# A weight conversion's integer scaling and a second value product given to GpSimd, with the converting periods in another order

## The chip, the cores and the metric

The kernel runs on one core of a Trainium2 chip. The metric is the time of one execution on the device in microseconds (us), as the median of several runs. A profile of one execution stands beside it, with every instruction's start and duration on TensorE (PE in the profile), VectorE (DVE), ScalarE (ACT), GpSimd (POOL) and the DMA queue of SyncE (SP).

## What is computed

The reference has two parts. The first is a threshold attention over 8 batches, 8 heads, 576 positions and 64 dimensions: scores are `q k^T / 8`; scores below the row's maximum less `tau` are dropped; what stays goes through exp, is divided by its row sum and multiplies `v`. The second part takes the result as 4608 rows of 512 and computes `relu(x @ w_in)**2 @ w_out` with `w_in` of 512 x 2048 and `w_out` of 2048 x 512.

```python
scores = scale * np.matmul(q, k.transpose(0, 1, 3, 2))
thresh = np.max(scores, axis=-1, keepdims=True) - tau
scores = np.where(scores >= thresh, scores, -1000000000.0)
attn = np.exp(scores - np.max(scores, axis=-1, keepdims=True))
attn = attn / (np.sum(attn, axis=-1, keepdims=True) + 1e-09)
h = np.maximum(x @ w_in, 0.0)     # x: the attention's output, heads side by side
out = (h * h @ w_out)
```

The two weight matrices arrive as float64 (they are made by multiplying float32 numbers by a float64 factor), so the kernel reads them as pairs of 32-bit words, a low and a high one, and makes float32 numbers of them with integer arithmetic.

## The kernel before, in words

The kernel has two stages. The attention goes first, in *periods*; the matrix products of the second part follow (lines 1117 to 1187), where a scheme of sums and differences of blocks saves products. The change touches the attention's periods alone.

**Periods.** Heads are taken in 32 pairs, and the query rows of two pairs make 9 units of 128 rows, 144 units in all. One call of `period(p)` (line 608) handles units A = 2p and B = 2p + 1: for each unit and each head j of the pair it makes scores (`SA`, `SB`), takes the row's extreme while it copies the scores from PSUM to SBUF (`topA0`, `topA1`, `topB0`, `topB1`, line 452, VectorE), makes the threshold on GpSimd (`leastA`, `leastB`, line 459, only 128x2 numbers), the exponentials on ScalarE (`powA0` and so on, line 462) and the mask with its row sum on VectorE (`maskA0` and so on, line 467: it reads the scores and the exponentials, both in SBUF). `over` (line 474, GpSimd) adds the small constant to the row sums of the period before and `inv` (line 477, VectorE) inverts them.

The same call works on earlier units too: `U`, `V` and `W` transpose the masked weights on TensorE into PSUM, `eU`, `eV` and `eW` copy them out on ScalarE (line 523); `W` also spreads the inverted sums (line 515). `PV` multiplies them by the values (line 532), and `x` takes the two heads' products out of PSUM: where no weights are converted, VectorE multiplies each by the inverted sums on the way (line 644). `T` and `eT` transpose a new pair's queries or keys (lines 398, 403 and 411).

**Conversion.** In periods 2 to 34 the kernel also converts 32 chunks of weights, one begun in each of periods 2 to 33 (`converts`, line 583). A chunk is 128 partitions of 512 numbers. `c1` (line 205, ScalarE) takes the magnitude of the high words, `c2` (line 212, ScalarE) scales the low words' integers in place, `c3` (line 219, GpSimd) clamps the magnitude, `c4` (line 227, VectorE) shifts and masks it, `c5` (line 235, VectorE) joins it with the high words' upper bits, `c6` (line 245, GpSimd) adds the scaled low words. `c1` and `c2` work on the chunk that the period begins, `c3` to `c6` on that of the period before. In converting periods `x` is split: ScalarE copies head 0's product (line 642) and GpSimd multiplies it later (`xm`, line 654), VectorE multiplies head 1's on the way out.

**Order.** Each engine runs its instructions in program order, and the program order within a period is a list of step names written out by hand: `PLAIN` (line 592) for periods without conversion, `CONVERTING` (line 597) for those with it. So one list sets the queue of every engine. Before the change, a converting period gives:

- VectorE: topA1 topA0 topB0 topB1 maskA1 inv maskA0 x(head 1) c4 maskB1 c5 maskB0
- GpSimd: over leastA leastB c3 c6 xm
- ScalarE: eU c1 c2 powA1 powA0 eV powB1 powB0 x(head 0) eT eW
- TensorE: U SA SB V PV T W

`touch` (line 355) adds waits between engines that use the same PSUM bank: the scores of unit A and `PV` share banks 0 and 5, the scores of unit B and `W` share banks 2 and 3, `T` and the last 64 keys of the scores share banks 1 and 4; `U` and `V` share one buffer.

Of the kernel before, what the change touches and what calls it, by code (L numbers as in the profile page):

```python
# [12 lines left out]
U32 = mybir.dt.uint32  # L13
ALU = mybir.AluOpType
AF = mybir.ActivationFunctionType
# [33 lines left out]
def kernel(  # L49
# [25 lines left out]
    nc = tc.nc  # L75
    B, H, S, D = q.shape
    P = 128
# [131 lines left out]
    def convert2(m):  # L209
        if m in parts:  # L210
            lo = parts[m][0]
            nc.scalar.activation(out=lo, in_=lo.bitcast(U32), func=AF.Copy, bias=0.0, scale=2.0**-29)

    def convert3(m):
        if m not in parts:
            return
        a = parts[m][2].bitcast(FP32)
        low, high = (0x38000000, 0x47EFFFFF)
        nc.gpsimd.tensor_scalar(  # L219
            out=a, in0=a, scalar1=as_float(high), scalar2=as_float(low), op0=ALU.min, op1=ALU.max  # L220
        )

    def convert4(m):
        if m not in parts:
            return
        lo, hi, a = parts[m]
        nc.vector.tensor_scalar(
            out=a, in0=a, scalar1=3, scalar2=0x3FFFFFFF, op0=ALU.logical_shift_left, op1=ALU.bitwise_and
        )
# [255 lines left out]
    wT = {}  # L485

    TURNS = {}
    for g in range(2, 2 * len(pairs)):
        two, x = divmod(g - 4, 4)
# [4 lines left out]
    SCALE_AT = 10  # L494
# [4 lines left out]
    def fill(m, f, pt, at=None):  # L499

        first, count = FILLS[f]
        if m not in wT:
            wT[m] = sb.tile([P, (2 * CH + 2) * P], FP32, tag="wT", bufs=W_RING, name="wT")
        for i, (u, c) in enumerate(FIRST[first : first + count]):
            half_turn(pt, i, weights[2 * m + u][:, c, :, :].rearrange("p j d -> p (j d)"), at)
        if f == "W":
            rs = smalls.pop(m)
            for j in range(2):
                for r in range(2):
                    rows = ds(r * HALF, HALF)  # L510
                    for u in range(2):
                        one = rs[rows, 3, 2 * u + j : 2 * u + j + 1]
                        wide = bass.AP(tensor=one.tensor, offset=one.offset, ap=[one.ap[0], [0, D]])
                        to = pt[ds(u * D, D), r, ts(count + j, HALF)]
                        made = nc.tensor.matmul(to, wide, ident[rows, rows], start=True, stop=True)  # L515
                        touch("turns", made, at and at + r * BANK, BANK)

    def filled(m, f, pt, at=None):

        first, count = FILLS[f]  # L520
        count += 2 * (f == "W")
        to = wT[m][:, ds(weight_at(first) * P, count * P)]
        touch("weights", nc.scalar.copy(joined(to), whole(pt, 0, count)), at, 2 * BANK, m)  # L523
# [15 lines left out]
    def valued(m):  # L539

        for u in range(2):
            n = 2 * m + u
            weights.pop(n)
            if units[n][1] == FULL:
                for i in units[n][0]:
                    loaded_v.pop(i)
                    if i + 3 < len(pairs):
                        load_v(i + 3)
# [10 lines left out]
    def has(n):  # L559
        return 0 <= n < NU  # L560
# [13 lines left out]
    def ask(every=True):  # L574

        while given:
            to, from_ = given.popleft()
            nc.sync.dma_start(out=to, in_=from_)
        for _ in range(len(later) if every else min(1, len(later))):
            to, from_ = later.popleft()  # L580
            nc.sync.dma_start(out=to, in_=from_)

    def converts(p):
        return is_wide and (has_chunk(p) or has_chunk(p - 1))

    def has_chunk(p):
        return p in starts

    def begun(n):
        return starts.get(n)  # L590
# [4 lines left out]
        maskB1  # L595
    """.split()
    CONVERTING = """
        fetch U SA s1 eU over topA1 topA0 leastA SB c1 topB0 V c2 PV topB1 powA1 powA0
        eV powB1 maskA1 T leastB inv c3 powB0 W maskA0 x c4 maskB1 c5 maskB0 c6 xm eT eW
    """.split()  # L600

    def spots():
        return [(sc[:, ds(b * BANK + REST, (FULL + 1) * HALF)], b * BANK) for b in (1, 4)]

    def middle():
        return sc[:, 2 * BANK : 4 * BANK].rearrange("p (r n) -> p r n", r=2)

    def period(p):

        A, B_, a, b = 2 * p, 2 * p + 1, 2 * p - 2, 2 * p - 1  # L610
        m, turns = p - 2, TURNS.get(p, ())
        late, pt = {"W": []}, {}

        def fills(f, m):
            if has(2 * m):
                pt[f] = pt_pool.tile([P, 2, BANK], FP32, tag="pt", name="pt")
                fill(m, f, pt[f])

        def evict(f, m):
            if has(2 * m):  # L620
                filled(m, f, pt[f], 2 * BANK if f == "W" else None)

        def W():
            if has(2 * m + 2):
                pt["W"] = middle()
                fill(m + 1, "W", pt["W"], 2 * BANK)

        def turn_some():
            late["turn"] = [turn(g // 2, g % 2, spots()) for g in turns]

        def PV():
            if has(2 * m):
                values(m)

        def values_out():
            if not has(2 * m):
                return
            late["x"] = x = sb.tile([P, 2, P], FP32, tag="x", bufs=2, name="x")
            for j in range(2):
                from_ = sc[:, ds(5 * j * BANK, P)]  # L640
                if converts(p) and j == 0:
                    made = nc.scalar.copy(x[:, j, :], from_)
                else:
                    made = nc.vector.tensor_tensor(  # L644
                        out=x[:, j, :], in0=from_, in1=wT[m][:, ts(SCALE_AT + j, P)], op=ALU.mult
                    )
                touch("x", made, 5 * j * BANK, P, m)

        def given_out():
            if has(2 * m):  # L650
                x = late.pop("x")
                if converts(p):
                    mine = x[:, 0, :]
                    nc.gpsimd.tensor_tensor(out=mine, in0=mine, in1=wT[m][:, ts(SCALE_AT, P)], op=ALU.mult)
                wT.pop(m)
                valued(m)
                give_x(m, x)
            ask(False)

        def scored_a():  # L660
            if has(A):
                scores(A, False)
                scores(A, True)
                scores(B_, True)
                softmax(A)

        def scored_b():
            if has(A):
                scores(B_, False)
                softmax(B_)  # L670

        def every(key):
            for then in late.get(key, ()):
                then()

        steps = {
            "U": lambda: fills("U", m), "V": lambda: fills("V", m + 1), "W": W, "T": turn_some,
            "eU": lambda: evict("U", m), "eV": lambda: evict("V", m + 1), "eW": lambda: evict("W", m + 1),
            "eT": lambda: every("turn"),
            "SA": scored_a, "SB": scored_b,  # L680
            "PV": PV, "x": values_out, "xm": given_out,
            "c1": lambda: convert1(begun(p)), "c2": lambda: convert2(begun(p)),
            "c3": lambda: convert3(begun(p - 1)), "c4": lambda: convert4(begun(p - 1)),
            "c5": lambda: convert5(begun(p - 1)), "c6": lambda: convert6(begun(p - 1)),
            "s1": lambda: sums_due(p) and sums_step(), "s2": lambda: sums_due(p) and p < 60 and sums_step(), "fetch": lambda: fetch(begun(p + 2)),
        }
        steps["over"] = lambda: do(a, "over")
        steps["inv"] = lambda: do(a, "inverse")
        for letter, n in (("A", A), ("B", B_)):
            for what, name in (("least", "least"),):  # L690
                steps[what + letter] = lambda n=n, name=name: do(n, name)
            for what, name in (("top", "top"), ("pow", "power"), ("mask", "mask")):
                for j in range(2):
                    steps[f"{what}{letter}{j}"] = lambda n=n, name=name, j=j: do(n, name, j)
        for name in CONVERTING if converts(p) else PLAIN:
            steps[name]()
        for n in (A, B_):
            if has(n) and units[n][1] == FULL:
                for i in units[n][0]:
                    turned.pop(i)  # L700
# [489 lines left out]
def as_float(bits):  # L1190
    import struct

    return struct.unpack("<f", struct.pack("<I", bits))[0]
# [30 lines left out]
```

## Time and profile before

| what | value |
|---|---|
| median of 3 runs | 1316.72 us (1316.07 to 1317.4) |
| the profiled execution's own time | 1314.57 us |
| span of its trace | 1312.8 us |
| busy share of the span: PE, DVE, ACT, POOL | 97%, 77%, 65%, 66% |
| converting periods | 33, from about 30 us to 269 us of the span |
| time of one converting period in the trace | 7.26 us (`inv` starts at 152.22 and 159.48 us) |

The shares are averages over two stages with different limits: the second stage, from about 520 us, keeps TensorE busy almost without a gap, and in the attention VectorE and ScalarE are as busy as TensorE. A row of a timeline gives the start, the duration, the engine, the line of the kernel, the operation, and in square brackets how long the engine had been idle and for whom it waited. Durations of neighbours on VectorE and ScalarE overlap at their ends, so the distance from start to start is what an instruction takes of its engine.

### The profile page before, as it was taken

Reading aid. Unit: us, or ns where it says so; the run is one execution under the profiler, and the core shown is the slowest. Engines: PE = TensorE matmul, PEld = TensorE weight load, DVE = VectorE, ACT = ScalarE, POOL = GpSimd, SP = SyncE. Lnnn points to the kernel's source line nnn. Section 1 sums busy time; section 2 is a strip of 40 time slices with the busy share of each in tenths; the row PEclk is TensorE's granted clock in tenths of the full one; section 3 lists DMA queues with packets and bytes.
Section 4 is the critical chain, followed back from the end, with each engine's and each line's share of the span. In section 5 each row is a group of like instructions: output and inputs, shape, how many; then the busy total and the mean of one; then the engine's idle time right before and its main releaser. Section 6 shows DMA issues by size and latency. Waiting matters only on the chain.

```text
span 1312.8 us, 47885 instructions
## 1 busy us (share of the span) xinstructions
PE 1271.9 (97%) x19483; PEld 1142.1 (87%) x19483; DVE 1007.1 (77%) x2464; ACT 855.8 (65%) x1497; POOL 872.0 (66%) x991
## 2 busy tenths in 40 slices
PE   8998989899999999999999999999999999999998
PEld 5666666677777777999999999999999999999998
DVE  5999999999999996877887788777656654665463
ACT  6999999988999986566756675665524322432240
POOL 1556555565555421778887888758777777777775
PEclk9999999999999999999999999999999999999999
DMA  5465566544433312466556655669745224522411
GB/s 150 105 176 153 153 177 179 153 113 103 99 78 84 79 42 47 148 209 198 183 184 209 200 188 176 194 229 387 260 161 161 63 99 162 161 65 97 161 33 33
DMA packets 247035, 192.12 MB, mean 146 GB/s; under 512 B 97184, under 2 KB 195488, under 8 KB 246816
## 3 DMA queue, kind: packets, MB, share of 16 engines
q1 hardware_dynamic: 245504, 188.66, 47.6%
q8 instruction: 153, 2.51, 0.8%
q14 instruction: 66, 0.54, 0.1%
q10 hardware_dynamic: 1312, 0.41, 0.1%
HBM read 116.65 MB, written 72.35 MB: 144 GB/s over the span
## 4 chain that ended last, share of the span: by engine, by line
PE 74%; DVE 7%; issue 6%; ACT 3%; POOL 3%; DMA 3%; SPq 0%; POOLq 0%; DVEq 0%; ACTq 0%
PE ph L825 30%; PE po L960 29%; PE sc L532 6%; PE sc L434 5%; DVE arena L452 4%; PE pt L380 3%; POOL arena L219 2%; DVE arena L467 2%; ACT arena L462 1%; ACT arena L523 1%; DVE arena L235 1%; PE sc L398 1%; DMA xT<-arena 1%; PE sc L515 1%; DMA wall<-w 1%
## 5 line engine op out<-in xcount | busy, mean ns | idle before, releaser
L125 POOL TENSOR_TENSOR arena<-arena 128x512 f32<-128x512 f32 (+1 forms) x314 | 378.1, 1223 | 133.6 <-DVE arena L125 115.8
L960 PE MATMUL po<-wall,arena 128*128 128x128 f32 x3528 | 394.8, 275 | 1.4 <-ACT arena L737 1.4
L960 PEld LDWEIGHTS po<-wall,arena 128*128 128x128 f32 x3528 | 394.3, 192 | 1.9 <-ACT arena L737 1.8
L825 PE MATMUL ph<-arena,wall 128*128 128x128 f32 x3528 | 394.2, 275 | 0.7 <-DVE arena L644 0.7
L825 PEld LDWEIGHTS ph<-arena,wall 128*128 128x128 f32 x3528 | 394.0, 192 | 0.8 <-issue 0.8
L125 DVE TENSOR_TENSOR arena<-ph,arena 128x512 f32<-128x512 f32 x378 | 256.4, 689 | 86.2 <-PE ph L825 65.4
L122 POOL TENSOR_TENSOR arena<-arena 128x128 f32<-128x128 f32 (+2 forms) x314 | 254.8, 812 | 49.1 <-DMA arena<-w 32.9
L125 DVE TENSOR_TENSOR arena<-po,arena 128x128 f32<-128x128 f32 x378 | 108.4, 290 | 167.8 <-PE po L960 163.4
L467 DVE SCALAR_TENSOR_TENSOR arena<-arena 128x576 f32<-128x576 f32 x288 | 229.5, 818 | 0.7 <-POOL arena L459 0.5
L462 ACT ACTIVATE arena<-arena 128x576 f32<-128x576 f32 x288 | 207.9, 772 | 15.6 <-DVE arena L452 11.4
L452 DVE TENSOR_SCALAR_CACHE_REDUCE arena<-sc 128x576 f32<-128x576 f32 x288 | 205.4, 751 | 15.8 <-ACT arena L523 4.6
L771 ACT COPY c<-arena 128x512 f32<-128x512 f32 (+1 forms) x303 | 174.0, 581 | 50.2 <-DVE arena L122 41.5
L532 PEld LDWEIGHTS sc<-arena 64*64 64x64 f32 x5760 | 153.7, 133 | 50.1 <-DVE arena L452 37.2
L532 PE MATMUL sc<-arena 64*64 64x128 f32 (+1 forms) x5760 | 169.8, 262 | 19.4 <-DVE arena L452 18.8
L122 DVE TENSOR_TENSOR arena<-arena,c 128x512 f32<-128x512 f32 (+1 forms) x267 | 175.1, 664 | 6.2 <-ACT c L771 4.1
L434 PE MATMUL sc<-arena 64*64 64x64 f32 (+1 forms) x2304 | 167.1, 414 | 6.7 <-ACT arena L403 4.0
L523 ACT COPY arena<-pt 128x1024 f32<-128x1024 f32 x144 | 146.1, 1015 | 27.0 <-PE pt L380 26.7
L737 ACT COPY arena<-po 128x128 f32<-128x128 f32 x63 | 16.7, 265 | 186.2 <-PE po L960 183.4
L459 POOL TENSOR_SCALAR arena<-arena,tau_p 128x2 f32<-128x2 f32 x144 | 74.8, 520 | 81.1 <-DVE arena L452 77.9
L380 PEld LDWEIGHTS pt<-ident,arena 64*128 64x128 f32 x2304 | 83.4, 138 | 43.9 <-ACT arena L523 27.5
L737 ACT COPY arena<-ph 128x512 f32<-128x512 f32 x63 | 36.7, 582 | 123.5 <-PE ph L825 122.9
L380 PE MATMUL pt<-ident,arena 64*128 64x64 f32 x2304 | 102.6, 228 | 5.9 <-ACT arena L523 4.7
(50 smaller groups left out, 892.0 us busy)
## 6 DMA issues: line engine op xcount, KB each, us to landing
g<-arena SPq DMA_DIRECT2D x144, 256.0 KB, 2.6
arena<-g SPq DMA_DIRECT2D x144, 256.0 KB, 4.4
w<-arena SPq DMA_DIRECT2D x60, 256.0 KB, 2.4
wall<-w SPq DMA_DIRECT2D x49, 256.0 KB, 5.2
arena<-w SPq DMA_DIRECT2D x44, 256.0 KB, 3.3
arena<-in_v_dram SPq DMA_DIRECT2D x32, 288.0 KB, 3.8
out_dram<-arena SPq DMA_DIRECT2D x70, 128.0 KB, 2.2
arena<-in_q_dram SPq DMA_DIRECT2D x64, 128.0 KB, 3.5
```

What stands on the lines that cost most here:

```text
L122: e.tensor_tensor(out=out, in0=x, in1=y, op=ALU.subtract)
L125: e.tensor_tensor(out=out, in0=x, in1=y, op=ALU.add)
L380: made = nc.tensor.transpose(pt[:, r, ts(slot, HALF)], of[rows, :], ident[rows, rows])
L434: made = nc.tensor.matmul(sc[at, ds(to, count)], lhs, kT[rows, ds(at_k, count)], start=True, stop=True)
L452: made = nc.vector.tensor_scalar(out=s[:, j, :], in0=sc[:, ds(at, S)], scalar1=1.0, scalar2=None, op0=ALU.mult, op1=ALU.min, accum_out=nmx ...
L462: nc.scalar.activation(out=w[:, :, j, :], in_=of(j), func=AF.Exp, bias=nmx[:, j : j + 1], scale=-1.0)
L467: nc.vector.scalar_tensor_tensor(out=w[:, :, j, :], in0=of(j), scalar=thr[:, j : j + 1], in1=w[:, :, j, :], op0=ALU.is_le, op1=ALU.mult, a ...
L523: touch("weights", nc.scalar.copy(joined(to), whole(pt, 0, count)), at, 2 * BANK, m)
L532: made = nc.tensor.matmul(sc[ds(u * D, D), ds(5 * j * BANK + row, count)], loaded_v[i][rows, (c - (u != j)) % CH, :], wT[m][rows, ds(weigh ...
L771: nc.scalar.copy(c, y)
L825: nc.tensor.matmul(to[:, j, :], W_IN[m, k][:, ts(j, P)], of[k][:, m - 1, :], start=(not more and j == 0), stop=True, skip_group_check=True,)
L960: nc.tensor.matmul(to, g[:, j, :], w[:, j, :], start=(not more and j == 0), stop=(j == 3), skip_group_check=True)
```

## The change

Four edits. `c2` becomes a GpSimd instruction with the same operands. In a converting period ScalarE copies both heads' products out of PSUM, and GpSimd's `xm` multiplies both (256 columns) by the inverted sums. `c3` clamps the chunk that the period itself begins, so it runs a period sooner than `c4`, which stays where it is. And the list `CONVERTING` has another order.

```diff
@@ convert2
-            nc.scalar.activation(out=lo, in_=lo.bitcast(U32), func=AF.Copy, bias=0.0, scale=2.0**-29)
+            nc.gpsimd.tensor_scalar(out=lo, in0=lo.bitcast(U32), scalar1=2.0**-29, scalar2=None, op0=ALU.mult)
@@ the order
     CONVERTING = """
-        fetch U SA s1 eU over topA1 topA0 leastA SB c1 topB0 V c2 PV topB1 powA1 powA0
-        eV powB1 maskA1 T leastB inv c3 powB0 W maskA0 x c4 maskB1 c5 maskB0 c6 xm eT eW
+        fetch SA U eU T SB topA0 s1 c1 topA1 topB0 c3 V PV leastA over powA0 topB1
+        powA1 powB0 c4 eT inv x maskA1 maskA0 W leastB maskB0 c5 eV c2 powB1 c6 eW maskB1 xm
     """.split()
@@ values_out
-                if converts(p) and j == 0:
+                if converts(p):
                     made = nc.scalar.copy(x[:, j, :], from_)
@@ given_out
                 if converts(p):
-                    mine = x[:, 0, :]
-                    nc.gpsimd.tensor_tensor(out=mine, in0=mine, in1=wT[m][:, ts(SCALE_AT, P)], op=ALU.mult)
+                    both = x[:, :, :].rearrange("p j n -> p (j n)")
+                    nc.gpsimd.tensor_tensor(out=both, in0=both, in1=wT[m][:, ds(SCALE_AT * P, 2 * P)], op=ALU.mult)
@@ steps
-            "c3": lambda: convert3(begun(p - 1)), "c4": lambda: convert4(begun(p - 1)),
+            "c3": lambda: convert3(begun(p)), "c4": lambda: convert4(begun(p - 1)),
```

The queues of a converting period after the change:

- VectorE: topA0 topA1 topB0 topB1 c4 inv maskA1 maskA0 maskB0 c5 maskB1
- GpSimd: c3 leastA over leastB c2 c6 xm
- ScalarE: eU c1 powA0 powA1 powB0 eT x(head 0) x(head 1) eV powB1 eW
- TensorE: SA U T SB V PV W

`convert2` has a second caller, `convert_out` (line 1057), but the list it works through is empty with these sizes (`EARLY` is 16, and there are 16 blocks).

## The prediction

> **What bounds the kernel now.** I read the page's first lines, then busy time by stretches, then the timelines of the engines in one converting period.
>
> ```profile
> span 1312.8 us, 47885 instructions
> ...
> core 0: us, PE busy (x) PEld busy (x) DVE busy (x) ACT busy (x) POOL busy (x), PEclk, DMA share, GB/s
> 140.00:180.00 40.00, 35.88 (x934) 25.31 (x930) 38.52 (x112) 39.47 (x69) 24.04 (x34) 1.00 0.63 171
> ```
>
> The second row names the columns. In these 40 us of converting periods ScalarE is busy 39.47, VectorE 38.52, TensorE 35.88 and GpSimd 24.04. So ScalarE and VectorE both look full, and shares can't say which of them sets the pace. VectorE's timeline of one period can.
>
> ```profile
> 151.48 0.82 DVE L467 SCALAR_TENSOR_TENSOR arena<-arena 128x576 f32<-128x576 f32 x1
> ...
> 152.22 0.17 DVE L477 RECIPROCAL arena<-arena 128x4 f32<-128x4 f32 x1
> 152.31 0.79 DVE L467 SCALAR_TENSOR_TENSOR arena<-arena 128x576 f32<-128x576 f32 x1
> ...
> 153.03 0.29 DVE L644 TENSOR_TENSOR arena<-sc,arena 128x128 f32<-128x128 f32 x1
> 153.61 0.43 DVE L227 TENSOR_SCALAR arena<-arena 128x512 int32<-128x512 int32 x1 [0.29 <-POOL arena L219]
> ...
> 153.95 0.81 DVE L467 SCALAR_TENSOR_TENSOR arena<-arena 128x576 f32<-128x576 f32 x1
> ...
> 155.29 0.81 DVE L467 SCALAR_TENSOR_TENSOR arena<-arena 128x576 f32<-128x576 f32 x1
> ...
> 156.03 0.75 DVE L452 TENSOR_SCALAR_CACHE_REDUCE arena<-sc 128x576 f32<-128x576 f32 x1
> ...
> 158.74 0.81 DVE L467 SCALAR_TENSOR_TENSOR arena<-arena 128x576 f32<-128x576 f32 x1
> ...
> 159.48 0.17 DVE L477 RECIPROCAL arena<-arena 128x4 f32<-128x4 f32 x1
> ```
>
> From `inv` (L477) to `inv` is 159.48 - 152.22 = 7.26 us. Everything follows its forerunner at once, except `c4` (L227), which waits 0.29 us for GpSimd's `c3`. VectorE's own work is thus 6.97 us. Two of its terms matter later: a mask (L467) takes 0.74 from start to start (155.29 to 156.03), and the four tops (L452) take 2.71 (156.03 to 158.74, where the next mask starts).
>
> ```profile
> 151.74 0.72 POOL L459 TENSOR_SCALAR arena<-arena,tau_p 128x2 f32<-128x2 f32 x1 [0.87 <-DVE arena L452]
> 152.43 1.15 POOL L219 TENSOR_SCALAR arena<-arena 128x512 f32<-128x512 f32 x1
> 155.46 1.54 POOL L245 TENSOR_TENSOR arena<-arena 128x512 int32<-128x512 int32 x1 [1.89 <-DVE arena L235]
> 156.97 0.45 POOL L654 TENSOR_TENSOR arena<-arena 128x128 f32<-128x128 f32 x1
> 157.51 0.23 POOL L474 TENSOR_SCALAR arena<-arena 128x4 f32<-128x4 f32 x1
> 157.83 0.29 POOL L459 TENSOR_SCALAR arena<-arena,tau_p 128x2 f32<-128x2 f32 x1
> ```
>
> GpSimd's `c3` (L219) comes behind `leastB` (L459), which waits for the last top: that is why `c4` waits. ScalarE follows:
>
> ```profile
> 155.41 0.73 ACT L205 ACTIVATE arena<-arena 128x512 f32<-128x512 f32 x1
> 156.00 0.73 ACT L212 ACTIVATE arena<-arena 128x512 int32<-128x512 uint32 x1
> 156.83 1.46 ACT L462 ACTIVATE arena<-arena 128x576 f32<-128x576 f32 x2
> ```
>
> `c2` (L212) ends at 156.73, and the powers start at 156.83, just after VectorE's first top (156.03 + 0.75 = 156.78). ScalarE is nearly full, but it follows VectorE. TensorE does too: a gap of 0.62 us stands ahead of `PV` (L532), ended by a top:
>
> ```profile
> 153.44 0.71 PE L380 MATMUL pt<-ident,arena 64*128 64x64 f32 x16
> 154.08 2.18 PE L434 MATMUL sc<-arena 64*64 64x512 f32 x32
> ...
> 157.53 2.20 PE L532 MATMUL sc<-arena 64*64 64x128 f32 x72 [0.62 <-DVE arena L452]
> ```
>
> So **VectorE with GpSimd's `c3`** is the bound, and the converting stage is the only one that the change touches.
>
> **What GpSimd costs VectorE.** The profile holds a coupling that the chain of waits doesn't name. At the end of conversion, GpSimd adds weights with 512-column sums (L122, L125) while VectorE wants to mask.
>
> ```profile
> 270.44 1.82 DVE L467 SCALAR_TENSOR_TENSOR arena<-arena 128x576 f32<-128x576 f32 x1 [0.52 <-POOL arena L459]
> ...
> 277.58 1.10 DVE L467 SCALAR_TENSOR_TENSOR arena<-arena 128x576 f32<-128x576 f32 x1
> ...
> 290.82 0.81 DVE L467 SCALAR_TENSOR_TENSOR arena<-arena 128x576 f32<-128x576 f32 x1
> ```
>
> ```profile
> 270.37 1.28 POOL L122 TENSOR_TENSOR wall<-wall 128x512 f32<-128x512 f32 x1
> ...
> 276.79 1.28 POOL L125 TENSOR_TENSOR wall<-wall 128x512 f32<-128x512 f32 x1
> ...
> 289.69 1.29 POOL L125 TENSOR_TENSOR wall<-wall 128x512 f32<-128x512 f32 x1
> ```
>
> A mask, which reads two operands from SBUF, takes 0.81 alone. The one at 270.44 starts 0.07 after a GpSimd sum and takes 1.82: it is held 1.01 us, until 271.45, 0.20 before the sum's end (271.65). The one at 277.58 is held 0.29, until 277.87, again 0.20 before that sum's end (278.07). At 290.82 the sum ends only 0.16 later, and the mask isn't held. The reverse holds too: `leastB` issued during a mask takes 0.72, `leastA` during the tops (which read PSUM) 0.29. `leastB` at 151.74 ends at 152.46, 0.24 after the mask let go at 152.22. So **GpSimd's instructions and VectorE's masks exclude one another**: whoever starts first keeps the other out. The Trainium skill says so (SBUF — State Buffer, "SBUF: two separate sides": a GpSimd instruction and a VectorE one with two SBUF inputs take an exclusive lock, and the loser blocks); the trace agrees, save that the lock goes 0.20 us before GpSimd's recorded end.
>
> Read so, `c3`'s 1.15 us is mostly waiting: issued at 152.43 under a mask that lets go at 153.03, it ends at 153.58. That is 0.55 after the release, so some 0.60 us unhindered, an estimate (`leastB` loses 0.05 the same way: 0.24 against 0.29). `c6`, issued under the mask of 155.29, ends at 157.00, 0.97 after that mask let go (156.03).
>
> **The change, part by part.**
>
> ```profile
> L122 POOL TENSOR_TENSOR arena<-arena 128x512 f32<-128x512 f32 x134 | 170.5, 1273 | 10.2
> L122 POOL TENSOR_TENSOR arena<-arena 128x128 f32<-128x128 f32 x176 | 80.2, 458 | 38.7 <-DMA arena<-w 32.9
> L644 DVE TENSOR_TENSOR arena<-sc,arena 128x128 f32<-128x128 f32 x111 | 28.5, 286 | 6.5 <-issue 4.3 <-PE sc L532 1.8
> L227 DVE TENSOR_SCALAR arena<-arena 128x512 int32<-128x512 int32 x32 | 13.7, 427 | 9.5 <-POOL arena L219 9.5
> L212 ACT ACTIVATE arena<-arena 128x512 int32<-128x512 uint32 x32 | 22.8, 712 | 0.0
> L642 ACT COPY arena<-sc 128x128 f32<-128x128 f32 x33 | 8.2, 249 | 0.0
> ```
>
> *VectorE's second `x` goes*: 33 converting periods (the count of L642) by 0.286 us (L644) = 9.4 us.
>
> *`c4` no longer waits for `c3`*, which ran a period earlier: its idle time in the row, 9.5 us.
>
> *ScalarE* loses `c2` (32 x 0.71) and gets 33 more copies of 0.25: 39.47 busy us in 40 are 7.16 a period, so 6.7 are left. Nothing is counted for this, since VectorE sets the pace; ScalarE and TensorE (35.88 in 40, so 6.5 a period) merely have to keep under the new period. They do: with `PV` started at the second top's end (1.4 us into the period, counted from the first top), it ends at 3.6; the two copies end at about 4.0, the scores of unit A (under 1.4 of the 2.18 us of both, L434) at 5.4, `U` (0.7, L380) and `T` (8 or 10 of the transposes of which `U` has 16, so at most 0.4) at 6.5, while the next first top, which the bank rule now makes wait for `T`, is due at 7. What hides the reordered ScalarE work is this 0.5 us; if it went, the period would grow by what is missing.
>
> *`xm` doubles to 256 columns.* Sums of 128 and 512 columns (0.458 and 1.273) give 0.00212 us a column, so 0.73 instead of 0.45. It follows `c6` while VectorE does its tops, which hold nobody out.
>
> *`c3`, `leastA`, `over` now stand ahead of `inv`.* That is an added wait: `inv` and behind it all masks now queue on VectorE for GpSimd. Counted from the first top: `c6` ends at 0.97 as now, `xm` at 1.67, `c3` (0.60, under the tops, its magnitude being made by then) at about 2.3, `leastA` at 2.6; `over` starts between 2.5 and 2.85 (gaps between GpSimd instructions are -0.03 to 0.09 in the rows above) and lasts 0.23. `inv` could start at 2.71 + 0.34 (`c4`'s step, 153.61 to 153.95) = 3.05. So `over` just makes it. I count 0.04 us a period for brushes with `c4` and `leastB`: 1.3 us.
>
> *`c2` on GpSimd* isn't in the trace. It comes behind `leastB`, with masks on VectorE until `c6`. It therefore can't run without holding a mask: issued during `maskA1`, it gets its turn when that ends and holds `maskA0` until 0.20 before its own end. That a waiting GpSimd instruction is let in between two masks was seen once: an `xm` issued under a mask took 1.07, and the mask behind that one 1.01 instead of 0.81, held until 31.05, 0.19 before `xm`'s end.
>
> ```profile
> 30.85 1.01 DVE L467 SCALAR_TENSOR_TENSOR arena<-arena 128x576 f32<-128x576 f32 x1
> ```
>
> ```profile
> 30.17 1.07 POOL L654 TENSOR_TENSOR arena<-arena 128x128 f32<-128x128 f32 x1 [0.83 <-ACT arena L642]
> ```
>
> `c2`'s length unhindered is bounded by `c3` (one input, 512 columns: 0.60) and a 512-column sum (1.28); below nothing it can't be, since it must read its 512 columns. I take `c3`'s, the same operation on as many numbers: after the release 0.55, less 0.20, holds a mask 0.35 us. 32 x 0.35 = **11.2 us**. A full sum's hold was 1.01 us at 270.44, the upper end: 32.3 us. `c6`, two integer inputs, gives 0.97 - 0.20 = 0.77, the middle.
>
> The skill has a rule against this edit (Perfetto Trace Analysis, "Optimizing Scalar/DVE Operations": moving work between VectorE and GpSimd might not help, since they share a port). By it the edit is a loss that the other edits must pay for, and that is how the sum treats it.
>
> *DMA queue*: the loads of queries and keys (issued at `eT`) now precede `c6`'s store instead of following `xm`'s; each still waits for its own producer and is needed a period or more later, so 0.
>
> The sum: -9.4 - 9.5 + 11.2 + 1.3 = -6.4 us. A period goes from 7.26 to 7.07. The profiled execution took 1314.57 (its span and 1.77 around it), 2.15 below the median of the runs shown; I apply the difference to the median: 1316.72 - 6.4 = **1310.3 us**.
>
> **The rivals.**
>
> *`c2` is dear* (the slower end). Its numbers are read as unsigned integers, scaled as floats and written as integers, two conversions that `c3` lacks, and the words lie two apart. Masks lose what it holds; the saving of 18.9 - 1.3 = 17.6 us is used up at 17.6 / 32 = 0.55 us of hold, a length of 0.80. At `c6`'s hold (0.77) it is 24.6 - 17.6 = +7.0: 1323.7 us; at the sum's, +14.7: 1331.4. For it: every GpSimd row with two inputs is slow. Against: `c3`, and `c2` has but one input. Chance 0.36.
>
> *`over` loses to `c4`.* If `c4` starts first and also keeps GpSimd out, `over` ends 0.2 after it, `inv` starts 0.2 later and `leastB` brushes a mask: 0.24 us more a period, 32 x 0.24 = 7.7: 1318.0 us, no gain, within what can be measured. For it: `over`'s start may fall either side of 2.71. Against: no row shows `c4` holding GpSimd. The skill's page SBUF — State Buffer ("The single rule" and its consequences) lists this kind of operation among those that can take the lock; that would give this rival's time. Chance 0.17.
>
> *`c3` really takes 1.15 us, and small integers hold nobody.* Then `over` ends at 3.5, `inv` waits 0.45, but `c2` is free: -18.9 + 32 x 0.45 = -4.5: 1312.2 us, also faster. For it: the row as printed. Against: the held masks. Chance 0.07.
>
> *The change doesn't do what it says*, ScalarE's relief being worthless: that is in the sum already, at nothing.
>
> **How the numbers follow.** The forecast has 0.40, "dear" 0.36, `over` behind `c4` 0.17, the third rival 0.07. Within 0.2% is 2.6 us, about what a measurement of this kernel can tell from no change. Faster: 0.39 of the forecast's 0.40 and 0.06 of the third's, 0.45. Slower: 0.33 of "dear" (the rest lies near its break-even) and 0.04 of the second's, 0.37. Same: what stays, 0.18. The range goes from 1305 (`c2`'s hold at 0.2 us, 32 x 0.15 = 4.8 under the forecast) to 1325, a little above `c6`'s price; it leaves out the upper half of "dear", 0.15, and little below.
>
> **What would show it.** `c4` without idle time, and L644 with 78 instructions instead of 111: the two savings. `c2`'s row on GpSimd: about 1.1 us as recorded, of which 0.5 is waiting, and one mask in each period stretched by 0.35 us (0.81 to 1.16). `inv` at most 0.1 us late behind `over`. If the stretched mask has 1.5 us or more, the first rival holds; if `inv` waits 0.2 and more, the second. It would be wrong altogether if first tops came to wait for TensorE or ScalarE, whose margin is 0.5 us a period.

## The result, and the profile after

| | before | after |
|---|---|---|
| median, all runs beside each other | 1316.93 us (4 runs, 1316.07 to 1317.4) | 1308.43 us (4 runs, 1307.46 to 1310.71) |
| profiled execution | 1314.57 us | 1308.12 us |
| period, `inv` to `inv` | 7.26 us | 7.06 us (156.42 to 163.48) |

The ratio is 0.9939 (95% interval 0.9921 to 0.9956), so 5.8 to 10.4 us faster. The forecast was 1310.3, a gain of 6.4; the two profiled executions differ by 6.45, the medians by 8.5, because the profiled execution of before lay 2.36 below the median of this table and that of after only 0.31. The gain comes from the converting periods: 29 of them, from `inv` at 43.32 to `inv` at 255.38, took 212.06 us before, and the same 29 (42.71 to 249.12) take 206.41 after, 5.65 less; behind the conversion the same `inv` comes at 296.68 instead of 303.69. Not every period is of the usual length: of the 29, two are longer before (8.57 and 7.46 us) and two after (7.65 and 7.77).

VectorE's timeline of one period after (start, duration, engine, line, operation):

```profile
153.37 0.75 DVE L452 TENSOR_SCALAR_CACHE_REDUCE arena<-sc 128x576 f32<-128x576 f32 x1
...
156.09 0.42 DVE L227 TENSOR_SCALAR arena<-arena 128x512 int32<-128x512 int32 x1
156.42 0.16 DVE L477 RECIPROCAL arena<-arena 128x4 f32<-128x4 f32 x1
156.51 0.78 DVE L467 SCALAR_TENSOR_TENSOR arena<-arena 128x576 f32<-128x576 f32 x1
...
157.22 1.19 DVE L467 SCALAR_TENSOR_TENSOR arena<-arena 128x576 f32<-128x576 f32 x1
...
158.35 0.81 DVE L467 SCALAR_TENSOR_TENSOR arena<-arena 128x576 f32<-128x576 f32 x1
...
163.48 0.17 DVE L477 RECIPROCAL arena<-arena 128x4 f32<-128x4 f32 x1
```

`c4` (L227) follows the last top without a wait, and `inv` (L477) follows `c4`. Head 1's product (L644) is gone. One mask, the second, takes 1.19 us instead of 0.81: from start to start 1.13 instead of 0.74. GpSimd's timeline beside it:

```profile
152.87 1.47 POOL L245 TENSOR_TENSOR arena<-arena 128x512 int32<-128x512 int32 x1 [1.14 <-DVE arena L235]
154.30 0.73 POOL L654 TENSOR_TENSOR arena<-arena 128x256 f32<-128x256 f32 x1
155.00 0.62 POOL L219 TENSOR_SCALAR arena<-arena 128x512 f32<-128x512 f32 x1
...
155.95 0.23 POOL L474 TENSOR_SCALAR arena<-arena 128x4 f32<-128x4 f32 x1
156.28 0.39 POOL L459 TENSOR_SCALAR arena<-arena,tau_p 128x2 f32<-128x2 f32 x1
156.74 2.03 POOL L212 TENSOR_SCALAR arena<-arena 128x512 int32<-128x512 uint32 x1
```

Counted from the first top at 153.37, `c6` ends at 0.97, `xm` at 1.66, `c3` at 2.25 (0.62 us long, no longer 1.15), and `over` (L474) starts at 2.58. Then `c2` (L212) stands under the masks for 2.03 us.

The groups, to set beside those of before; the first row, of the masks, is from the view of before, the others are from after:

```profile
L467 DVE SCALAR_TENSOR_TENSOR arena<-arena 128x576 f32<-128x576 f32 x288 | 229.5, 818 | 0.7 <-POOL arena L459 0.5
...
L644 DVE TENSOR_TENSOR arena<-sc,arena 128x128 f32<-128x128 f32 x78 | 19.0, 285 | 6.6 <-issue 4.3 <-PE sc L532 1.8
L227 DVE TENSOR_SCALAR arena<-arena 128x512 int32<-128x512 int32 x32 | 13.5, 422 | 0.0
L212 POOL TENSOR_SCALAR arena<-arena 128x512 int32<-128x512 uint32 x32 | 65.1, 2035 | 2.5
L467 DVE SCALAR_TENSOR_TENSOR arena<-arena 128x576 f32<-128x576 f32 x288 | 237.4, 860 | 1.3 <-POOL arena L459 0.8 <-ACT arena L462 0.4
```

L644 has 33 instructions less, `c4` no idle time at all. The masks' mean rises from 818 to 860 ns, so 288 x 0.042 = 12.1 us have gone into masks that were held.

### The profile page after: what moved, and what is told of

The parts are those of the page before. It is cut to its first block, busy times and chain, and to the rows that moved or that the text cites. A ratio compares the mean times of both kernels' runs of the same rounds, so it can differ in the third digit from the quotient of the medians.

```text
span 1306.3 us, 47872 instructions
## 1 busy us (share of the span) xinstructions
PE 1284.5 (98%) x19483; PEld 1159.8 (89%) x19483; DVE 1010.8 (77%) x2431; ACT 845.7 (65%) x1498; POOL 916.4 (70%) x1023
## 4 chain that ended last, share of the span: by engine, by line
PE 87%; ACT 5%; DMA 3%; DVE 3%; issue 1%; POOL 1%; SPq 0%; ACTq 0%; DVEq 0%; POOLq 0%
PE po L960 29%; PE ph L825 28%; PE sc L532 11%; PE sc L434 10%; PE pt L380 5%; DVE arena L452 3%; ACT arena L462 2%; PE sc L515 2%; DMA wall<-w 2%; PE sc L398 2%; ACT arena L523 1%; PE sc L380 1%; DMA g<-arena 1%; ACT arena L403 0%; ACT c L771 0%
## 5 line engine op out<-in xcount | busy, mean ns | idle before, releaser
L467 DVE SCALAR_TENSOR_TENSOR arena<-arena 128x576 f32<-128x576 f32 x288 | 237.4, 860 | 1.3 <-POOL arena L459 0.8
L532 PEld LDWEIGHTS sc<-arena 64*64 64x64 f32 x5760 | 159.2, 133 | 36.7 <-DVE arena L452 20.2
L532 PE MATMUL sc<-arena 64*64 64x128 f32 (+1 forms) x5760 | 180.8, 262 | 2.7 <-DVE arena L452 1.3
L434 PE MATMUL sc<-arena 64*64 64x64 f32 (+1 forms) x2304 | 176.9, 414 | 6.2 <-ACT arena L403 4.2
L434 PEld LDWEIGHTS sc<-arena 64*64 64x64 f32 x2304 | 74.3, 134 | 45.1 <-ACT arena L403 15.1
```

The lines of the kernel that those rows point to most:

```text
L434: made = nc.tensor.matmul(sc[at, ds(to, count)], lhs, kT[rows, ds(at_k, count)], start=True, stop=True)
L467: nc.vector.scalar_tensor_tensor(out=w[:, :, j, :], in0=of(j), scalar=thr[:, j : j + 1], in1=w[:, :, j, :], op0=ALU.is_le, op1=ALU.mult, a ...
L532: made = nc.tensor.matmul(sc[ds(u * D, D), ds(5 * j * BANK + row, count)], loaded_v[i][rows, (c - (u != j)) % CH, :], wT[m][rows, ds(weigh ...
```

## The experiments

**The theory.** VectorE sets the converting period. Its own work there is 6.97 - 0.29 = 6.68 us, what before had less the product; the period is that, and whatever holds a mask or makes VectorE late. (From start to start the product takes 0.21 and `c4`'s wait took 0.37, as the end of a product overlaps with what follows; the sum of the two, 0.58, is the same.) **A rival** comes from the chain of waits of the profile, whose first row reads, before and then after:

```profile
PE 74%; DVE 7%; issue 6%; ACT 3%; POOL 3%; DMA 3%; SPq 0%; POOLq 0%; DVEq 0%; ACTq 0%
...
PE 87%; ACT 5%; DMA 3%; DVE 3%; issue 1%; POOL 1%; SPq 0%; ACTq 0%; DVEq 0%; POOLq 0%
```

It puts 87% of the chain on TensorE, where it was 74%. And in the row of the converting stage that answers to the one shown of before (PE first, then PEld, DVE, ACT, POOL) TensorE is busy 39.56 of 40 us, like VectorE with 40.00:

```profile
140.00:180.00 40.00, 39.56 (x984) 30.01 (x984) 40.00 (x109) 38.42 (x71) 32.77 (x42) 1.00 0.65 172
```

So perhaps the period of 7.07 us is TensorE's, and `c2` costs nothing. All ratios below are to the kernel before, run on the same chip; the changed kernel's is 0.9939.

**1. `c2` left out** (`e1_no_c2`).

```diff
-            nc.gpsimd.tensor_scalar(out=lo, in0=lo.bitcast(U32), scalar1=2.0**-29, scalar2=None, op0=ALU.mult)
+            pass
...
-        nc.gpsimd.tensor_tensor(out=a, in0=hi, in1=lo, op=ALU.add)
+        nc.gpsimd.tensor_tensor(out=a, in0=hi, in1=spare[0], op=ALU.add)
```

`spare[0]` is a tile of 512 zeros on each partition, filled once; the low words are left out.

> Leaves out c2: the low words aren't scaled, c6 adds zeros from a spare tile. Theory: VectorE sets the converting period, and c2 costs it a hold of 0.37 to 0.40 us of one mask in each; without it no mask is stretched, the period goes from 7.07 to about 6.70, and 32 periods give 12 us: about 1296.5 us (9 us if TensorE, at 6.5 to 6.8 us a period, then comes up). Rival: TensorE has become the bound (it is busy 39.6 of 40 us, and 87% of the chain that ended last is its own): taking c2 away moves the time by less than 2 us.

Measured: 1306.73 us, 0.993 (0.9909 to 0.9952), as if the rival were right. The timelines say otherwise. GpSimd and VectorE about one `inv`:

```profile
153.60 0.28 POOL L459 TENSOR_SCALAR arena<-arena,tau_p 128x2 f32<-128x2 f32 x1
153.95 0.38 POOL L474 TENSOR_SCALAR arena<-arena 128x4 f32<-128x4 f32 x1
```

```profile
153.82 0.42 DVE L227 TENSOR_SCALAR arena<-arena 128x512 int32<-128x512 int32 x1
154.36 0.18 DVE L477 RECIPROCAL arena<-arena 128x4 f32<-128x4 f32 x1
```

No mask is held by `c2` any more, but `c6`, reading its zeros from another tile, took longer: it ended 1.23 us after the last mask let go in this period, 0.97 in the changed kernel (1.90 and 1.47 as recorded). So `over` started at 153.95, after `c4`. It took 0.38 instead of 0.23, and `inv` came at 154.36, not 154.16: 6.68 + 0.20 = 6.88 us, the period that was measured. This is the second rival of the prediction, with the 0.2 us that it gave for `inv`, and it shows that `c4` stretches a GpSimd instruction that meets it, as the masks do. Beside that, seven periods of some 8 us ate up the rest (run 3 shows how).

**2. The same, with `c6`'s zeros spaced like the low words** (`e1b_no_c2`: `in1=pick(spare[0], 0)`, a tile among the weights).

> Leaves out c2 again, but c6 reads its zeros with the same spacing as the low words. In e1 the masks were not stretched any more, yet c6 ended 1.24 us after the last mask let go instead of 0.97, over then fell behind c4 and inv came 0.2 us late (6.88 us a period), and 8 periods slipped by 1 us when the last mask came late and c6 went first. Theory (VectorE and GpSimd's queue set the period): with c6 as before, over is in time and the period is 6.70 us, apart from slips: 1296 to 1302 us. Rival (TensorE is the bound, at 6.88 us): the period stays at 6.85 to 6.9.

Measured: 1313.03 us, 0.9972 (0.9961 to 0.9983). Both expectations missed: `c6` grew again.

```profile
149.50 2.03 POOL L245 TENSOR_TENSOR wall<-arena,wall 128x512 int32<-128x512 int32 x1 [2.82 <-DMA arena<-in_k_dram]
```

```profile
152.79 0.46 DVE L227 TENSOR_SCALAR arena<-arena 128x512 int32<-128x512 int32 x1
153.65 0.18 DVE L477 RECIPROCAL arena<-arena 128x4 f32<-128x4 f32 x1 [0.41 <-POOL arena L474]
```

With `c6` at 2.03 us, `inv` starts 153.65 - 152.79 - 0.34 = 0.52 us late, and 6.68 + 0.52 = 7.20 is the period measured. So the time of `inv` explains this period too. That alone doesn't show what set 6.88 in the run before: the run that I wanted needed `c6` untouched.

**3. A fair pair: no loads, with and without `c2`** (`e11_no_fetch` and `e1c_no_c2_no_fetch`). The weight words aren't loaded, four tiles are zeroed once (so all weights come out zero), and `c6` reads the same words as in the changed kernel.

```diff
-        nc.sync.dma_start(out=three(raw[:, :]), in_=src.bitcast(I32))
+        if m < 4:
+            nc.gpsimd.memset(raw[:, :].bitcast(FP32), 0.0)
```

> The changed kernel with the loads of the weight words left out (four tiles are zeroed once instead, so all weights are zero): the yardstick for the next run. Both theories: 7.07 us a period, within 4 us of the changed kernel, since only transfers go.

> The same without c2: c6 now reads the very words that it reads in the changed kernel (in e1 and e1b another tile under c6 made it 0.3 and 0.5 us longer, and inv late by 0.20 and 0.52). Theory: a mask gets back its 0.37 to 0.40 us, 6.68 to 6.72 us a period, 11 to 12 us less than the run without loads. Rival (TensorE is the bound): 6.85 us and more, under 7 us less.

Measured: 1307.83 us, 0.9943 (0.9927 to 0.996), with a period of 7.07; and without `c2` 1304.94 us, 0.992 (0.9902 to 0.9938). The time is 2.9 us less, not 11: by the total the rival would have been right. But of 31 periods without `c2` twenty-two take 6.67 to 6.90 us, twenty of them 6.67 to 6.75, and nine take 7.69. VectorE without `c2`, a short period and a long one:

```profile
147.87 0.17 DVE L478 RECIPROCAL arena<-arena 128x4 f32<-128x4 f32 x1
...
154.60 0.17 DVE L478 RECIPROCAL arena<-arena 128x4 f32<-128x4 f32 x1
...
156.88 0.69 DVE L236 SCALAR_TENSOR_TENSOR arena<-arena 128x512 int32<-128x512 int32 x1
157.63 1.69 DVE L468 SCALAR_TENSOR_TENSOR arena<-arena 128x576 f32<-128x576 f32 x1
...
162.29 0.16 DVE L478 RECIPROCAL arena<-arena 128x4 f32<-128x4 f32 x1
```

```profile
156.75 0.84 ACT L463 ACTIVATE arena<-arena 128x576 f32<-128x576 f32 x1
```

```profile
157.66 1.04 POOL L246 TENSOR_TENSOR arena<-arena 128x512 int32<-128x512 int32 x1 [2.81 <-DVE arena L236]
```

The period of 6.73 us (147.87 to 154.60) settles it against TensorE: with all its work it can go about as fast as VectorE's own 6.68. (ScalarE has no room left there: in most of the short periods the last mask starts 0.03 to 0.04 us behind the end of its exponentials, and up to 0.08 later than VectorE could have begun it.) In the next one the last mask is due at 157.48 (0.60 after `c5`, L236), but its exponentials (L463) are ready only at 157.59. The mask starts at 157.63, but in the gap `c6` has got in and holds it until 158.50, 0.20 before `c6`'s end: 0.15 us of lateness has become 1.0 (the next instruction starts at 159.24, and was due at 158.22). So `c2`'s hold of 0.39 us is a real price, and at the same time the slack in which ScalarE's last exponentials come in time: taking it away gains some 0.37 us in 22 periods and loses 7.69 - 7.07 = 0.62 in nine, -8.1 + 5.6 = -2.5 us.

**4. `c3` on the chunk of the period before** (`e2_c3_late`: `"c3": lambda: convert3(begun(p - 1))`).

> The changed kernel, but c3 clamps the chunk of the period before again, at its new place ahead of leastA. Theory: what freed c4 is the place at the head of GpSimd's queue (c3 ends about 2.3 us into the period, c4 starts at 2.7), not the period: c4 has no idle time and the total stays within 1.5 us. Rival: the clamp a period sooner is what did it: c4 waits again, 0.3 us in 32 periods, +9.5 us.

Measured: 1309.35 us, 0.9955 (0.9941 to 0.9968), which overlaps the changed kernel's interval; the period is 7.07. The row of `c4`:

```profile
L227 DVE TENSOR_SCALAR arena<-arena 128x512 int32<-128x512 int32 x32 | 13.3, 416 | 0.0
```

No idle time. The place of `c3` at the head of GpSimd's queue is enough to free `c4`; that it runs a period sooner is worth nothing in this order.

**5. `c2` on ScalarE again** (`e3_c2_act`: the old `nc.scalar.activation` line, behind `eV`).

> The changed kernel, but c2 on ScalarE again, at its place behind eV. Theory: no mask is stretched any more, but ScalarE gets 0.6 us a period back, 6.7 + 0.6 = 7.3, and so becomes the bound itself: a period of 7.2 to 7.35, +4 to +9 us. Rival: ScalarE only follows, so its relief is worth nothing and the masks' 0.37 us is all that counts: a period of 6.7 to 6.8, -9 to -12 us.

Measured: 1325.78 us, 1.0077 (1.0054 to 1.0099), a period of 7.68: the right sign, and more than twice the size. The row of the stage (PE, PEld, DVE, ACT, POOL), and ScalarE, VectorE and GpSimd around the last mask:

```profile
140.00:180.00 40.00, 36.94 (x900) 27.45 (x904) 37.99 (x100) 38.87 (x70) 19.84 (x33) 1.00 0.61 160
```

```profile
151.72 0.71 ACT L212 ACTIVATE arena<-arena 128x512 int32<-128x512 uint32 x1
152.31 0.79 ACT L462 ACTIVATE arena<-arena 128x576 f32<-128x576 f32 x1
```

```profile
152.07 0.68 DVE L235 SCALAR_TENSOR_TENSOR arena<-arena 128x512 int32<-128x512 int32 x1
153.13 1.37 DVE L467 SCALAR_TENSOR_TENSOR arena<-arena 128x576 f32<-128x576 f32 x1 [0.38 <-ACT arena L462]
...
154.42 0.75 DVE L452 TENSOR_SCALAR_CACHE_REDUCE arena<-sc 128x576 f32<-128x576 f32 x1
```

```profile
152.84 1.04 POOL L245 TENSOR_TENSOR wall<-arena 128x512 int32<-128x512 int32 x1 [2.81 <-DMA arena<-in_k_dram]
```

The mask is due at 152.67 and starts at 153.13, since `c2` stands ahead of its exponentials; `c6` goes first, and from the mask's start to the next instruction's it is 1.29 instead of 0.74. 6.68 + 0.46 + 0.55 = 7.69. So ScalarE is late at one place, in every period, and VectorE pays twice. Whether ScalarE would also be the bound by its work alone, as I had expected, this run can't tell: it is busy 38.87 of 40 us, an estimated 7.46 of the 7.68, and without `c6`'s 0.55 VectorE would need only 7.14.

**6. Head 1's product on VectorE again** (`e4_x_dve`: the split of before, with `x` behind `maskA0`).

> The changed kernel, but head 1's product is multiplied by VectorE on its way out of PSUM again (behind maskA0), and xm has 128 columns. Theory: 0.29 us of VectorE come back in each of 33 periods: a period of 7.36, +9.4 us; the shorter xm gives nothing, since over is early enough already. Rival: TensorE or ScalarE sets the period by now, and VectorE's 0.29 us find room: less than +4 us.

Measured: 1321.19 us, 1.0036 (1.0025 to 1.0048), 7.55 to 7.62 us in most periods, where I had expected 7.36. Two rows of its waits (from 60 to 250 us; in total, times, longest):

```profile
PEld sc L434 <- DVE arena L644: 19.8, 26, 0.8
DVE arena L452 <- PE sc L398: 5.2, 21, 0.3
```

VectorE's 0.21 us (from the product's start to the next) come back, and more: the next scores wait on TensorE for VectorE's multiplication instead of ScalarE's copy (19.8 us in 26 waits, about 0.8 each), `T` comes late, and the first top waits for it, 0.2 to 0.3 us. 6.68 + 0.39 + 0.21 + 0.29 = 7.57.

**7. The edits without the order** (`e7_old_order`: the old `CONVERTING` list).

> The three edits in the old order of steps. Theory: c2 then starts under the tops and holds no mask, but c3, behind leastB, starts under the masks and holds one for 0.35 to 0.4 us in its place, c4 waits for nobody (its chunk was clamped a period earlier): 7.05 to 7.15 us a period, within 3 us of the changed kernel. Rival: the new order is what makes the edits pay: a period above 7.26, +6 us and more over the changed kernel.

Measured: 1319.72 us, 1.0023 (1.0013 to 1.0034), 7.42 us a period: slower than before, so my expectation fell and its rival held. VectorE and GpSimd:

```profile
155.11 1.00 DVE L467 SCALAR_TENSOR_TENSOR arena<-arena 128x576 f32<-128x576 f32 x1
...
156.85 0.42 DVE L227 TENSOR_SCALAR arena<-arena 128x512 int32<-128x512 int32 x1
157.38 1.15 DVE L467 SCALAR_TENSOR_TENSOR arena<-arena 128x576 f32<-128x576 f32 x1
...
158.47 0.68 DVE L235 SCALAR_TENSOR_TENSOR arena<-arena 128x512 int32<-128x512 int32 x1
```

```profile
154.84 1.61 POOL L212 TENSOR_SCALAR arena<-arena 128x512 int32<-128x512 uint32 x1
156.55 0.80 POOL L459 TENSOR_SCALAR arena<-arena,tau_p 128x2 f32<-128x2 f32 x1
157.32 0.61 POOL L219 TENSOR_SCALAR arena<-arena 128x512 f32<-128x512 f32 x1
```

`c2` starts late under the tops and still holds the first mask 0.20 us (0.94 from start to start, with `inv` at 156.05); `leastB` behind it is late, so that the third mask starts at 157.38 instead of 157.19; and `c3` holds that mask 0.35. 6.68 + 0.20 + 0.19 + 0.35 = 7.42. I had counted only the last. `c4` follows the mask before it without a wait (156.85): with `c3` in its old place, that it runs a period sooner is enough to free `c4`.

One longer period of this run shows how long `c2` holds a mask:

```profile
200.92 0.81 DVE L467 SCALAR_TENSOR_TENSOR arena<-arena 128x576 f32<-128x576 f32 x1
...
201.66 0.17 DVE L477 RECIPROCAL arena<-arena 128x4 f32<-128x4 f32 x1
```

`c2` runs there from 200.11 to 201.73. The mask starts 0.81 us later than `c2`, lies wholly beside it and takes its usual 0.74. So the hold lies at the head of `c2`, and isn't spread over it.

**8. The order without the edits** (`e8_order_only`).

> The kernel before with the new order of steps alone (c2 on ScalarE, head 1's product on VectorE, c3 on the chunk of the period before). Theory: c4 no longer waits (c3 is early), but head 1's product now stands between inv and maskA1 and waits there for PV, which ends some 3.65 us into the period: 0.29 us of work and 0.5 of waiting on VectorE give 7.4 to 7.7 us a period, 1321 to 1331 us. Rival: the order is good by itself: below 7.26 us, under 1316.

Measured: 1323.21 us, 1.0063 (1.0044 to 1.0083), 7.53 us a period, as expected.

```profile
157.10 0.17 DVE L477 RECIPROCAL arena<-arena 128x4 f32<-128x4 f32 x1
157.94 0.29 DVE L644 TENSOR_TENSOR arena<-sc,arena 128x128 f32<-128x128 f32 x1 [0.67 <-PE sc L532]
```

The product waits 0.67 us there for `PV`. Neither half of the change pays alone: the order needs VectorE free of the product, the edits need GpSimd's queue in the new order.

**9. `c2` under the tops** (`e9_c2_in_tops`: `... topB0 c3 c2 V ...`).

> The changed kernel, but c2 stands right behind c3 in GpSimd's queue, so that it begins under the tops, where nothing keeps it out. Theory: of c2's 2.04 us as recorded 0.48 are waiting for a mask and some 1.55 its own, of which only the first 0.4 hold a mask: it is recorded with 1.5 to 1.6, no mask is stretched, and leastA, over and inv come 1.4 us late: a period of 8.1, +33 us. Rival: c2 is as short as c3 (0.6) and its 2.04 are waiting behind two masks: it is recorded with 0.6 to 0.7 and the period is 7.2 to 7.3, +6 us.

Measured: 1344.9 us, 1.0213 (1.0196 to 1.023), a period of 8.29, a little more than the 8.1 expected.

```profile
151.29 1.64 POOL L212 TENSOR_SCALAR arena<-arena 128x512 int32<-128x512 uint32 x1
```

```profile
151.68 0.60 DVE L227 TENSOR_SCALAR arena<-arena 128x512 int32<-128x512 int32 x1
153.64 0.18 DVE L477 RECIPROCAL arena<-arena 128x4 f32<-128x4 f32 x1 [1.36 <-POOL arena L474]
```

Unhindered, `c2` takes 1.64 us. It stretches `c4` from 0.42 to 0.60; read as a hold at `c2`'s head, it holds VectorE until 151.86, 0.57 us from its start, although it runs on until 152.93. `inv` is 153.64 - 151.68 - 0.34 = 1.62 late, and 6.68 + 1.62 = 8.30.

**10. `c2` without conversions** (`e5_c2_f32`: float32 high words in, float32 zeros out).

> c2 without conversions: it multiplies the high words, read as float32 with the same spacing, by zero and writes float32 zeros over the low words, which c6 adds (so the low words are left out). Theory: the conversions from and to integers make c2 long: its row falls from 2.04 to about 1.1 (0.5 of it waiting, as forecast), while the stretched mask (its reading) stays at 1.15 to 1.2 and the time within 2 us of the changed kernel. Rival: the spacing of the words makes it long: 1.9 to 2.1 stays.

Measured: 1308.64 us, 0.9934 (0.9918 to 0.995), a period of 7.07.

```profile
155.95 2.15 POOL L212 TENSOR_SCALAR arena<-arena 128x512 f32<-128x512 f32 x1
```

It isn't the conversions, and the rival held. What is left is the spacing of the words (`c3`, dense, takes 0.61); a dense `c2` was not run, so this stays an inference.

**11. A version meant to be better** (`e10_powB1_first`: `c5 powB1 c2 eV c6`).

> The changed kernel with powB1 ahead of eV on ScalarE. Where powB1 is late, c6 gets in ahead of maskB1 and holds it (seen in e1 and, in every period, in e3). Theory: the period stays at 7.07 us, and slips of 0.6 to 1.7 us, of which the profiles of the changed kernel and of e2 show two and three, get fewer: 0 to 3 us faster than the changed kernel. Rival: eV, and with it U and the next first top, come late: a period of 7.2 and more, +4 us.

Measured: 1308.44 us, 0.9953 (0.9939 to 0.9967): the changed kernel's time. No last mask waits for its exponentials any more, but many periods take 7.10 to 7.16: `U` waits for the later `eV` (0.27 us in the period from 135.55), and the first top starts a little late behind `T` (0.09 there). Not better.

## Why the prediction was right, and where it was not

One sum describes all these kernels: VectorE's own 6.68 us, what holds it, and what makes it late. The terms are read from each kernel's own trace, so that the sums close shows only that nothing else made VectorE wait. The test of the theory is the second row, which was forecast as 6.68 to 6.72.

| kernel | own work and what was seen | sum | measured |
|---|---|---|---|
| changed | 6.68 + 0.39 (`c2`) | 7.07 | 7.07 |
| `e1c`, short periods | 6.68 | 6.68 | 6.67 to 6.75 |
| `e1` | 6.68 + 0.20 (`inv`) | 6.88 | 6.88 |
| `e1b` | 6.68 + 0.52 (`inv`) | 7.20 | 7.20 |
| `e9` | 6.68 + 1.62 (`inv`) | 8.30 | 8.29 |
| `e4` | 6.68 + 0.39 (`c2`) + 0.21 (product) + 0.29 (`T`) | 7.57 | 7.55 to 7.62 |
| `e3` | 6.68 + 0.46 (late) + 0.55 (`c6`) | 7.69 | 7.68 |
| `e7` | 6.68 + 0.20 + 0.19 + 0.35 | 7.42 | 7.42 |

Point by point:

- *What bounds the kernel*: right. The chain of waits named TensorE, but 6.73 us without `c2` shows that it had room.
- *Head 1's product, 9.4 us*: right as work (L644 has 33 less). From start to start it is 0.21 us, 6.9 in all, and what is missing is in `c4`'s wait, so the two together are the 18.9 of the sum. Undoing it cost more, because the scores wait for it.
- *`c4`'s wait, 9.5 us*: right. I put it down to `c3` running a period earlier, which is enough by itself (run 7); in the new order `c3`'s place is enough as well (run 4).
- *`c3`, unhindered, 0.60*: 0.62 measured. The reading that 1.15 us were mostly waiting was right, and the third rival falls with it.
- *`over` just makes it*: it starts at 2.58 of the forecast 2.5 to 2.85. The second rival's mechanism is real (run 1); in the changed kernel `inv` waits for `over` once between 60 and 250 us, 0.49 us in the period of 7.77, where `c3` had come late behind `c1`. The 1.3 us counted for brushes don't show: 6.68 and `c2`'s 0.39 make up the whole period.
- *`c2` holds a mask 0.35 us, 11.2 us in all*: measured 0.39, 12.1 us by the masks' mean. But the working behind it failed. I took `c2` to be as long as `c3`, 0.60, and to hold until 0.20 before its end; it is 1.64 long, and holds only about its first half microsecond (0.46 to 0.50 in run 7, 0.54 to 0.59 in run 9; 0.39 once it is let in). By my own rule a `c2` of 1.64 would have made the kernel slower (the break-even was 0.80): two errors that cancelled. That this term, and with it the total, came out right was luck. The forecast of its row, 1.1 us, was wrong for the same reason: 2.04.
- *ScalarE's relief, counted at nothing*: right as long as the rest stands; run 5 shows what it covers: with `c2` back on ScalarE the last mask is late in each period. By my own figures ScalarE, 7.16 us a period before, would have had 7.4 with the second copy and without this relief, above the old 7.26: `c2` had to go for the copy to fit.
- *TensorE and ScalarE have 0.5 us of room*: their room at the first top was enough in all periods but one between 60 and 250 us, that of 7.65 us, where the top waits 0.50 us for `T` after a pause on TensorE whose cause the trace doesn't name. The room at the last mask I had not looked at: from the end of its exponentials to its start it is 0.09 to 0.59 us, and in 9 of the 32 periods less than `c2`'s hold of 0.39 (0.10 and 0.34 in two: the exponentials end at 152.54 and 159.35, the masks start at 152.64 and 159.69). Without the hold it runs out.

The Trainium skill's rule (Perfetto Trace Analysis, "Optimizing Scalar/DVE Operations") that moving work between VectorE and GpSimd might not help agrees with run 7 (edits in the old order: 1.0023) and not with the changed kernel (0.9939): the order decides. It bears on head 1's multiplication alone, which went from VectorE to GpSimd; `c2`, to which the prediction applied it, came from ScalarE. That one-input operations on GpSimd run roughly at line rate (GPSIMD Engine Reference, "Engine selection") agrees with `c3` (512 columns in 0.61 us, beside 0.69 for ScalarE's `c1` on as many) and not with `c2` (1.64).

## What to carry to other kernels

Where two engines shut each other out, time a moved instruction twice: how long it is, and how long it holds the other; what runs beside it pays only the second, what waits behind it in its own queue pays the first (1.62 us in run 9). Place such instructions beside work that isn't shut out, here the tops (from start to start they took 0.68 us with GpSimd's `c6`, `xm` and `c3` beside them), and look at what they stand ahead of in their own queue. And look for places where an instruction that comes a tenth of a microsecond late lets a long one go first: there a small slip costs a whole hold.

## What the runs showed of the hardware that I had not expected

- A GpSimd instruction need not keep VectorE out until it ends. The 512-column sums did so until 0.20 us before their end, the spaced `c2` only for the first 0.46 to 0.59 of its 1.64 us; a mask that started 0.81 us into it wasn't held (run 7).
- `c4`, a VectorE instruction with one input, takes part too: it stretched `over` from 0.23 to 0.38 (run 1) and was itself stretched from 0.42 to 0.60 by `c2` (run 9).
- `c6` with the high and the low words of one tile took 1.04 us when it went first (run 5), and as recorded under a mask 1.47; with dense zeros from another tile 1.81 to 1.90, and spaced ones from a third place 2.03. Whether the place, the spacing or the zeros do it stays open.
- Who goes first is decided within a few hundredths: in run 3 a mask recorded at 157.63 was held by a `c6` recorded at 157.66.
